# GLA recurrence and SoLU block on one core: a group's first scores moved to another PSUM bank, weight conversion shifted by half a piece, and alpha's transposes moved forward

## The chip, the core and the metric

The kernel runs on one core of a Trainium2 chip. The metric is the device time of one execution in microseconds (us). Six runs of the kernel before gave 390.94 to 396.51 us, with a median of 394.48 us. One further execution was profiled: it took 391.19 us, of which 389.3 us lie between its first and its last instruction. All times inside the kernel below are counted from the first instruction of that execution.

Five engines work side by side, each through its own queue: TensorE (PE) multiplies matrices into PSUM banks, VectorE (DVE), ScalarE (ACT) and GpSimd (POOL) work element by element, and SyncE (SP) issues most of the DMA transfers.

## The reference

Inputs are q, k, v and alpha, each of 4 batches, 8 heads, 768 positions and 48 features, and the weights of a feed-forward block with a hidden width of 1024.

```python
for t in range(S):
    state = alpha[:, :, t, :, None] * state + np.einsum('bhd,bhe->bhde', k[:, :, t], v[:, :, t])
    y[:, :, t] = np.einsum('bhd,bhde->bhe', q[:, :, t], state)
...
x = np.ascontiguousarray(attn_out.transpose(0, 2, 1, 3)).reshape(B * S, H * D)
...
h = x @ w_in
h_max = np.max(h, axis=-1, keepdims=True)
e = np.exp(h - h_max)
sm = e / (np.sum(e, axis=-1, keepdims=True) + 1e-09)
solu = h * sm
mu = np.mean(solu, axis=-1, keepdims=True)
var = np.mean((solu - mu) ** 2, axis=-1, keepdims=True)
ln = (solu - mu) / np.sqrt(var + 1e-06) * g_ln
return (ln @ w_out).astype(np.float32)
```

The first part is a linear attention whose state decays by alpha; the second is an up projection, the product of h and its softmax, a normalisation over the hidden width, and a down projection.

## The kernel before: how it is tiled and ordered

The 768 positions are cut into 6 **groups** of 128. In a group, all 4 batches and 8 heads are worked on together: the running products of alpha are made by scans (`scan_back`, `scan_on`), they scale the transposed keys (`kT`) and queries (`qv`, and `qe` for the last 16 features of each head), and the scores of 4 heads at a time (`scores(g, half)`) are made by 64 small matmuls into four PSUM banks `a[0]` to `a[3]`, one for each batch. `masked(half)` multiplies the four banks by a triangular mask on DVE and so writes `sT`. Then the old state (`read_state`) and the values (`read_values`) are added up in PSUM and copied to `x`.

The feed-forward block of a group runs over 8 **blocks** f of 128 hidden units. `up_mm(g, f)` makes h of 512 tokens on PE, in one of the two banks of the pool `ps_h`. `up_act(g, f)` then issues three operations: e = exp(h) on ACT (L403), u = h*e on DVE (L404), and u2 = u*u on ACT (L405). The next block but one can only be written into the bank when L404 has read it. For group 0 the sums of e and u2 over the blocks are made on PE by `array_sums`, after the fourth and the eighth block. `down(n, half)` multiplies u by half of `w_out`; n counts batches of 128 tokens, and `finish(n)` scales and stores.

The schedule is written out by hand: every engine executes its instructions in the order in which the Python code issues them, and waits on semaphores for what the others must have done. A tile of a pool waits until the tile that held its bank has been read.

**Conversion of the weights.** The weights come as 64-bit floats. They are fetched in 8 **pieces** (`fetch`, onto the slots of the tile `room`; 0 to 3 belong to `w_in`, 4 to 7 to `w_out`), and made into 32-bit floats by `bits(i)` on DVE. It has two halves: part 0 is L594 and L597 (`top`), part 1 is L602, L605 and L606 (`low`, and the sum). `in_range(i)` squares and exponentiates a piece on ACT for a later check (L581, L582), and `scaled(i)` multiplies two blocks of `w_out` by the gains (L613). A slot may be fetched into again when `bits` and `in_range` have read it. Pieces 2 and 3 share slots 1 and 2.

**The stretch that the change touches** is the script between lines 712 and 809, which runs once: the 8 up blocks of group 0 (32 to 60 us), in whose shadow pieces 2 to 5 are converted and the inputs of group 1 are fetched, and then the preparation of group 1 (60 to 112 us). In the loop of the 8 up blocks, part f % 2 of piece 2 + f // 2 is converted after block f. Behind odd blocks (1, 3, 5) ACT has an `in_range` to do. After the loop come `bits(6)`, `bits(7)`, the token sums, the transposes of alpha (`alpha_T(1)`, two DVE transposes at L195 and L198, and a small memset on POOL), and then, three times, a backward scan followed by a product with the transposed keys `tk[i]`. On PE, group 0's `down` runs in pieces between the transposes of keys (`tk`) and queries (`tq`), the mean of `w_out` (`mean`), and `keys_back`. The queries `tq[0]` and `tq[1]` are held in the banks a0 and a1 until DVE multiplies them into `qv` (L780), `tq[1]` last of all. `scores(1, 0)` then takes a0 to a3 anew.

From line 813 on, groups 2 to 5 are worked off by a table (`attend`), which calls `alpha_T` too.

Of the kernel before, what the change touches and what calls it, by code (L numbers as in the profile page):

```python
# [32 lines left out]
def fast_path(ctx, tc, q, k, v, alpha, moe_w_in, moe_w_out, moe_g_ln, out):  # L33
# [12 lines left out]
    nc = tc.nc  # L46
    B, H, S, D = q.shape
# [5 lines left out]
    NB = H + NP  # L53
# [8 lines left out]
    def pool(name, bufs, **kw):  # L62
        return ctx.enter_context(tc.tile_pool(name=name, bufs=bufs, **kw))
# [8 lines left out]
    ps_h = pool("ps_h", 2, space=PS)  # L72
    ps_o = pool("ps_o", 2, space=PS)
    ps_a = pool("ps_a", 1, space=PS)
# [25 lines left out]
    an = const.tile([P, H, TQ, D], FP, name="an")  # L100
    qn = const.tile([P, H, TQ, D], FP, name="qn")
# [16 lines left out]
    SW = P + 1  # L118
    aT = const.tile([P, NB, SW], FP, name="aT")
# [25 lines left out]
    def by_token(x):  # L145

        return x.rearrange("p h u d -> p (h u d)").rearrange("p (b h d) -> p b h d", b=B, h=H)
# [9 lines left out]
    def ends_of(src, tag=None):  # L157

        ends = ring.tile([P, T4], FP, name=tag) if tag else two.tile([P, T4], FP, tag="two", name="ends")
        ends = ends.rearrange("p (b d) -> p b d", b=B)  # L160
        nc.scalar.copy(out=ends.rearrange("p b (h d) -> p b h d", h=H), in_=by_token(src)[:, :, :, E0:D])
        return ends
# [31 lines left out]
    def firsts(src, dst):  # L194
        nc.vector.transpose(out=dst.rearrange("p h (t u) -> p h u t", u=TQ), in_=src[:, :, :, 0:E0])  # L195

    def lasts(src, dst):
        nc.vector.transpose(  # L198
            out=dst.rearrange("p j (i t u) -> p u j i t", u=TQ, i=2),
            in_=src[:, :, :, E0:D].rearrange("p (j i) u d -> p u j i d", i=2),  # L200
        )

    def alpha_T(g):
        nc.gpsimd.memset(aT[:, :, 0:1], 0.0)
        firsts(an, aT[:, 0:H, 1:SW])
        lasts(an, aT[:, H:NB, 1:SW])

    def alpha_over(g):
        x = an.rearrange("p h u d -> p (h u d)")
# [60 lines left out]
    def quarter(b):  # L270
        return slice(32 * b, 32 * b + 32)

    def banks(name, shape, n=B):
        return [ps_a.tile([P] + shape, FP, tag=f"a{b}", name=f"{name}{b}") for b in range(n)]

    def scores(g, half, a=None):
        a = a or banks("a", [NP, P])
        for i in range(NP):
            h = half * NP + i
            for kb, qb in ((h, h), (H + h // 2, H + h)):  # L280
                for b in range(B):
                    nc.tensor.matmul(  # L282
                        a[b][:, i], lhsT=kT[quarter(b), kb], rhs=qv[quarter(b), qb], start=kb == h, stop=kb != h,
                        tile_position=(32 * b, 0), skip_group_check=True,
                    )
        masks[half] = a
# [98 lines left out]
    def up_mm(g, f):  # L385
        d = gr[g]
        h = ps_h.tile([P, T4], FP, tag="h", name="h")
        for a in range(KC):
            nc.tensor.matmul(  # L389
                h, lhsT=w_in[:, a, f * P : (f + 1) * P], rhs=d["x"][:, a].rearrange("p b t -> p (b t)"),  # L390
                start=(a == 0), stop=(a == KC - 1),
            )
        d["h"] = h
# [29 lines left out]
    def array_sums(g, half):  # L423


        d = gr[g]
        if half == 0:
            d["q"] = [ps_a.tile([P, T4], FP, tag=f"a{i}", name=f"quarters{i}") for i in range(2)]
        for i in range(2):
            for f in range(4):  # L430
                r = quarter(f)
                nc.tensor.matmul(
                    d["q"][i][r], lhsT=ones[:, 0:32], rhs=d[4 * half + f][i], start=half == 0, stop=half == 1,
                    tile_position=(0, r.start), skip_group_check=True,
                )
        if half:
            d["p"] = one.tile([P, 2, T4], FP, name="p")
            for i in range(2):
                nc.scalar.copy(out=d["p"][:, i], in_=d["q"][i])
            d["unit"] = small_ones  # L440
# [104 lines left out]
    def place(i):  # L545
        kind, f = pieces[i]
        return w_out[:, f : f + 2, 0:DM] if kind else w_in[:, :, f * P : f * P + 2 * P]
# [3 lines left out]
    def fetch(i, slot, n=1):  # L551

        kind, f = pieces[i]
        w = n * F // (2 if kind else KC)
        raw = room[:, 1536 * slot : 1536 * (slot + n)].bitcast(U32).rearrange("p (c f w) -> p c f w", f=w, w=2)
        if kind:
            parts = [(slice(0, P), c, moe_w_out[(f + c) * P : (f + c + 1) * P, :]) for c in range(2)]
        else:
            rows = moe_w_in[:, f * P : f * P + w].rearrange("(h d) f -> h d f", d=D)
            parts = [(slice(E0 * r, E0 * r + E0), c, rows[NP * c + r, 0:E0]) for c in range(2) for r in range(NP)]  # L560
            parts += [(slice(E1 * h, E1 * h + E1), 2, rows[h, E0:D]) for h in range(H)]
        for rows, c, src in parts:
            if float64:
                nc.sync.dma_start(out=raw[rows, c].rearrange("p f w -> p (f w)"), in_=src.bitcast(U32))  # L564
            else:
                dst = w_out[rows, f + c, 0:DM] if kind else w_in[rows, c, f * P : f * P + w]
                nc.sync.dma_start(out=dst, in_=src)
        for m in range(n):
            raws[i + m] = raw[:, :, w // n * m : w // n * (m + 1)]
# [14 lines left out]
    def bits(i, part=None):  # L584
        if not float64:
            return
        lo, hi = raws[i][:, :, :, 0], raws[i][:, :, :, 1]
        if part != 1:
            made[i] = [
                two.tile([P, F], FP, tag="two", name=x).rearrange("p (c f) -> p c f", c=hi.shape[1])  # L590
                for x in ("top", "low")
            ]
            top = made[i][0].bitcast(U32)
            nc.vector.tensor_scalar(  # L594
                out=top, in0=hi, scalar1=3, scalar2=0x3FFFFFF8, op0=ALU.logical_shift_left, op1=ALU.bitwise_and
            )
            nc.vector.scalar_tensor_tensor(  # L597
                out=top, in0=hi, scalar=0xC0000000, in1=top, op0=ALU.bitwise_and, op1=ALU.bitwise_or
            )
        if part != 0:  # L600
            top, low = made.pop(i)
            nc.vector.tensor_scalar(  # L602
                out=low.bitcast(U32), in0=top.bitcast(U32), scalar1=0xFF800000, scalar2=None, op0=ALU.bitwise_and
            )
            nc.vector.scalar_tensor_tensor(out=low, in0=lo, scalar=2.0**-52, in1=low, op0=ALU.mult, op1=ALU.mult)  # L605
            nc.vector.tensor_tensor(out=place(i), in0=low, in1=top, op=ALU.add)  # L606

    def scaled(i):

        f = pieces[i][1]  # L610
        for c in range(f, f + 2):
            w = w_out[:, c, 0:DM]
            nc.scalar.mul(out=w, in_=w, mul=g_col[:, c : c + 1])  # L613
# [55 lines left out]
    def three(name, where):  # L669
        return [pool.tile([P, NP, P], FP, tag=tag, name=f"{name}{i}") for i, (pool, tag) in enumerate(where)]  # L670
# [12 lines left out]
    for i in range(3):  # L683
        part = slice(NP * i, NP * i + NP)
# [4 lines left out]
    for i in (2, 0, 1):  # L689
        if i == 1:  # L690
            scan_on(0, i)
        part = slice(NP * i, NP * i + NP)
# [17 lines left out]
    in_range(1)  # L710

    for f in range(FC):
        p = 2 + f // 2
        up_mm(0, f)
        if f == 4:
            array_sums(0, 0)
        up_act(0, f)
        bits(p, f % 2)
        if f == 0:
            next_state(0)  # L720
            fetch(4, 3)
            load_first(k, kn, 1)
            load_first(q, qn, 1)
            load(alpha, an, 1)
        elif f == 1:
            in_range(2)
        elif f == 2:
            ends_k = ends_of(kn, "e")
        elif f == 3:
            in_range(3)  # L730
            ends_q = ends_of(qn, "u2")
        elif f == 4:
            fetch(5, 1)
            fetch(6, 2)
        elif f == 5:
            in_range(4)
            fetch(7, 3)
            load_v(1)
        elif f == 6:
            scaled(4)  # L740
        elif f == 7:
            scaled(5)
    bits(6)
    tk = three("tp_k", [(ps_a, "a2"), (ps_a, "a3"), (ps_h, "h")])
    turned(kn, ends_k, tk)
    load(k, kn, 2)
# [2 lines left out]
    scaled(6)  # L749
    bits(7)  # L750
    token_sums(0)
    alpha_T(1)
    down(1, 0)
    scaled(7)
    tq = three("tp_q", [(ps_a, "a0"), (ps_a, "a1")])
# [3 lines left out]
    for i in range(3):  # L759
        scan_back(1, i)  # L760
        part = slice(NP * i, NP * i + NP)
# [15 lines left out]
    for i in range(2):  # L777
        scan_on(1, i)
        part = slice(NP * i, NP * i + NP)
        nc.vector.tensor_tensor(out=qv[:, part], in0=tq[i], in1=aT[:, part, 1:SW], op=ALU.mult)  # L780
    down(2, 0)
    scores(1, 0)
    finish(1)
    alpha_over(1)
    load(alpha, an, 2)
# [3 lines left out]
    masked(1)  # L789
    finish(2)  # L790
    alpha_T(2)
    read_begin()
    for batches in ((0, 1), (2, 3)):
# [82 lines left out]
    for g in range(1, G + 1):  # L876
# [10 lines left out]
        for s in range(FC):  # L887
# [17 lines left out]
            if step:  # L905
                n, half = step
# [499 lines left out]
```

## Time and profile before

| what | us |
|---|---|
| median of 6 runs | 394.48 |
| the profiled execution | 391.19 |
| its span | 389.3 |
| PE busy in the span | 370.8 (95%) |
| DVE busy in the span | 250.5 (64%) |
| ACT busy in the span | 143.9 (37%) |
| 30 to 60 us: PE, DVE, ACT busy | 28.75, 25.48, 22.52 |
| 60 to 90 us: PE, DVE, ACT busy | 25.26, 28.42, 15.01 |
| share of DMA engines busy, 30 to 60 us | 0.89 |

A row of the timeline gives start and duration in us, engine, source line, operation, output <- inputs with their shapes, how many instructions were merged into the row, and in square brackets how long the engine stood idle just before and what ended the wait. Rows of one engine can overlap a little[...]. The chain of waits follows the execution back from its last instruction, at each step to what released it; its shares say on which engine and line the span was spent.

### The profile page before, as it was taken

Reading aid. Unit: us, or ns where it says so; the run is one execution under the profiler, and the core shown is the slowest. Engines: PE = TensorE matmul, PEld = TensorE weight load, DVE = VectorE, ACT = ScalarE, POOL = GpSimd, SP = SyncE. Lnnn points to the kernel's source line nnn. Section 1 sums busy time; section 2 is a strip of 40 time slices with the busy share of each in tenths; the row PEclk is TensorE's granted clock in tenths of the full one; section 3 lists DMA queues with packets and bytes.
Section 4 is the critical chain, followed back from the end, with each engine's and each line's share of the span. In section 5 each row is a group of like instructions: output and inputs, shape, how many; then the busy total and the mean of one; then the engine's idle time right before and its main releaser. Section 6 shows DMA issues by size and latency. Waiting matters only on the chain.

```text
span 389.3 us, 10598 instructions
## 1 busy us (share of the span) xinstructions
PE 370.8 (95%) x4661; PEld 224.1 (58%) x4661; DVE 250.5 (64%) x417; ACT 143.9 (37%) x252; POOL 125.0 (32%) x135
## 2 busy tenths in 40 slices
PE   8698999787999999999999999999999999999995
PEld 8685345455665556556656556566555575555552
DVE  0989888996987857694655893665895511444410
ACT  2628775553424325224253215153123231333111
POOL 4020000041042993337423436422635620333210
PEclk9989999999899999999999999999999999999999
DMA  9975989403446300674000764000600000000011
GB/s 183 195 192 158 231 269 163 94 20 86 111 113 83 83 3 3 82 184 102 22 2 24 112 155 101 22 3 22 101 2 22 22 24 2 20 21 21 22 43 48
DMA packets 86567, 30.79 MB, mean 79 GB/s; under 512 B 68072, under 2 KB 84720, under 8 KB 86512
## 3 DMA queue, kind: packets, MB, share of 16 engines
q1 hardware_dynamic: 85488, 29.11, 34.7%
q10 hardware_dynamic: 1024, 0.92, 0.7%
q8 instruction: 38, 0.62, 0.7%
q14 instruction: 17, 0.14, 0.1%
HBM read 25.30 MB, written 4.72 MB: 77 GB/s over the span
## 4 chain that ended last, share of the span: by engine, by line
PE 71%; DVE 12%; DMA 6%; ACT 5%; SPq 3%; issue 2%; DVEq 0%
PE o L500 30%; PE h L389 24%; PE y L314 9%; PE a L282 5%; DMA room<-in_v_dram 3%; SPq L152 2%; DMA room<-in_moe_w_in_dram 2%; DVE room L404 2%; PE kv L364 1%; ACT sq L581 1%; DVE aT L220 1%; SPq L564 1%; DMA kn<-in_k_dram 1%; DVE top L597 1%; DVE hT L220 1%
## 5 line engine op out<-in xcount | busy, mean ns | idle before, releaser
L500 PE MATMUL o<-w_out,room 128*128 128x385 f32 x384 | 135.0, 496 | 1.1 <-DVE least L234 1.1
L389 PE MATMUL h<-x,w_in 128*128 128x512 f32 x288 | 132.2, 598 | 1.2 <-DVE g_col L618 1.2
L500 PEld LDWEIGHTS o<-w_out,room 128*128 128x128 f32 x384 | 72.1, 192 | 58.1 <-issue 17.2
L389 PEld LDWEIGHTS h<-x,w_in 128*128 128x128 f32 x288 | 53.0, 189 | 59.9 <-issue 48.7
L404 DVE TENSOR_TENSOR room<-h,e 128x512 f32<-128x512 f32 x40 | 27.8, 694 | 83.0 <-ACT e L403 82.8
L403 ACT ACTIVATE e<-h 128x512 f32<-128x512 f32 x40 | 23.9, 598 | 105.5 <-PE h L389 105.5
L530 POOL TENSOR_TENSOR r<-sums,mhalf 128x1 f32<-128x1 f32 x20 | 14.3, 716 | 138.8 <-DVE sums L522 138.8
L420 POOL TENSOR_TENSOR p<-p,e 128x512 f32<-128x512 f32 x30 | 41.8, 1392 | 15.7 <-ACT e L403 15.6
L405 ACT ACTIVATE u<-room 128x512 f32<-128x512 f32 x40 | 25.2, 630 | 42.3 <-DVE room L404 42.3
L293 DVE TENSOR_TENSOR sT<-a,mask 128x512 f32<-128x512 f32 x44 | 27.3, 681 | 10.1 <-PE a L282 10.1
L282 PE MATMUL a<-qv,kT 32*128 32x128 f32 x704 | 27.7, 290 | 4.3 <-DVE least L234 1.9
L282 PEld LDWEIGHTS a<-qv,kT 32*128 32x128 f32 x704 | 24.2, 197 | 11.8 <-issue 4.0
L220 DVE TENSOR_TENSOR_SCAN hT<-aT,unit 128x516 f32<-128x516 f32 x18 | 23.1, 1337 | 8.6 <-ACT aT L677 8.5
L420 DVE TENSOR_TENSOR p<-p,u 128x512 f32<-128x512 f32 x30 | 23.2, 775 | 6.5 <-ACT u L405 6.5
L244 POOL TENSOR_TENSOR kT<-kT,hT 128x1024 f32<-128x1024 f32 (+1 forms) x8 | 13.3, 1685 | 42.8 <-DVE kT L195 42.8
L314 PE MATMUL y<-sT,vn 128*32 128x128 f32 x768 | 23.2, 274 | 2.0 <-issue 1.2
L220 DVE TENSOR_TENSOR_SCAN aT<-aT,seed 128x516 f32<-128x516 f32 x18 | 23.0, 1278 | 0.6
L314 PEld LDWEIGHTS y<-sT,vn 128*32 128x32 f32 x768 | 20.8, 110 | 3.9 <-issue 2.7
L212 ACT ACTIVATE sq<-an,mone 128x1536 uint8<-128x1536 f32 x12 | 18.8, 1570 | 0.2
L314 PE MATMUL y<-qv,state 32*32 32x128 f32 x960 | 16.9, 277 | 1.0 <-DVE sT L293 0.9
L314 PEld LDWEIGHTS y<-qv,state 32*32 32x32 f32 x960 | 12.1, 103 | 7.9 <-issue 5.4
L532 ACT ACTIVATE o_sb<-o,r 128x384 f32<-128x384 f32 x16 | 9.3, 582 | 18.8 <-POOL r L530 18.8
(141 smaller groups left out, 377.9 us busy)
## 6 DMA issues: line engine op xcount, KB each, us to landing
an<-in_alpha_dram SPq DMA_DIRECT2D x20, 192.0 KB, 4.8
out_dram<-o_sb SPq DMA_DIRECT2D x20, 192.0 KB, 1.9
room<-in_moe_w_out_dram SPq DMA_DIRECT2D x8, 384.0 KB, 4.8
kn<-in_k_dram SPq DMA_DIRECT2D x16, 192.0 KB, 4.1
qn<-in_q_dram SPq DMA_DIRECT2D x16, 192.0 KB, 4.1
vn<-in_v_dram SPq DMA_DIRECT2D x10, 256.0 KB, 3.9
room<-in_moe_w_in_dram SPq DMA_DIRECT2D x16, 128.0 KB, 3.9
kn<-in_k_dram SPq DMA_DIRECT2D x4, 384.0 KB, 5.8
```

What stands on the lines that cost most here:

```text
L212: nc.scalar.activation(out=sq, in_=x, func=AF.Relu, scale=sign, bias=mone, accum_out=over[:, g, i : i + 1])
L220: nc.vector.tensor_tensor_scan(out=o, data0=a, data1=s, initial=1.0, op0=ALU.mult, op1=ALU.add)
L282: nc.tensor.matmul(a[b][:, i], lhsT=kT[quarter(b), kb], rhs=qv[quarter(b), qb], start=kb == h, stop=kb != h, tile_position=(32 * b, 0), sk ...
L293: nc.vector.tensor_tensor(out=sT[:, b, half * NP : half * NP + NP], in0=a[b], in1=mask[:, None, :].to_broadcast([P, NP, P]), op=ALU.mult,)
L314: nc.tensor.matmul(y_bank(b)[quarter(r), a], lhsT=lhsT, rhs=rhs, start=(b, r) not in begun, stop=stop, tile_position=(row, 32 * r), skip_g ...
L389: nc.tensor.matmul(h, lhsT=w_in[:, a, f * P : (f + 1) * P], rhs=d["x"][:, a].rearrange("p b t -> p (b t)"), start=(a == 0), stop=(a == KC ...
L403: nc.scalar.activation(out=e, in_=h, func=AF.Exp)
L404: nc.vector.tensor_tensor(out=u, in0=h, in1=e, op=ALU.mult)
L405: nc.scalar.activation(out=u2, in_=u, func=AF.Square)
L420: eng.tensor_tensor(out=p, in0=d[0][i] if f == 1 else p, in1=d[f][i], op=ALU.add)
L500: nc.tensor.matmul(d["o"][:, 0 : DM + 1], lhsT=u_of(g, f)[:, b * P : b * P + P], rhs=w_out[:, f], start=(f == 0), stop=(f == FC - 1), skip ...
L530: nc.gpsimd.tensor_tensor(out=r, in0=s[:, 3:4], in1=mhalf, op=ALU.pow)
```

## The change

Four things are done, all of them in the order of the hand-written script; no operation is added or taken out.

1. In the loop of group 0's up blocks, both halves of piece 2 are converted after block 0, and from then on the conversion is half a piece ahead: part 0 of the next piece after odd blocks, part 1 after even ones. Piece 6's first half is converted after block 7, and only its second half after the loop.
2. `alpha_T` can be called in two parts. Part 0 is the memset and the transpose of the last 16 features (L198), part 1 the transpose of the first 32 (L195). For group 1, part 0 is issued after block 6, and part 1 after block 7, between the two halves of piece 6. For the other groups the two transposes change places.
3. `fetch(5, 1)` and `fetch(6, 2)` are issued after block 3, ahead of the copy `ends_q`, instead of after block 4.
4. `scores(1, 0)` gets a bank of `ps_h` in place of a1.

```diff
-    def alpha_T(g):
-        nc.gpsimd.memset(aT[:, :, 0:1], 0.0)
-        firsts(an, aT[:, 0:H, 1:SW])
-        lasts(an, aT[:, H:NB, 1:SW])
+    def alpha_T(g, part=None):
+        if part != 1:
+            nc.gpsimd.memset(aT[:, :, 0:1], 0.0)
+            lasts(an, aT[:, H:NB, 1:SW])
+        if part != 0:
+            firsts(an, aT[:, 0:H, 1:SW])
...
     for f in range(FC):
-        p = 2 + f // 2
         up_mm(0, f)
         if f == 4:
             array_sums(0, 0)
         up_act(0, f)
-        bits(p, f % 2)
+
+        for half in (0, 1) if f == 0 else (f + 1,):
+            bits(2 + half // 2, half % 2)
...
         elif f == 3:
             in_range(3)
-            ends_q = ends_of(qn, "u2")
-        elif f == 4:
             fetch(5, 1)
             fetch(6, 2)
+            ends_q = ends_of(qn, "u2")
...
         elif f == 6:
             scaled(4)
+            alpha_T(1, 0)
         elif f == 7:
             scaled(5)
-    bits(6)
+            alpha_T(1, 1)
+    bits(6, 1)
...
     token_sums(0)
-    alpha_T(1)
     down(1, 0)
...
     down(2, 0)
-    scores(1, 0)
+
+    scores(1, 0, three("a", [(ps_a, "a0"), (ps_h, "h"), (ps_a, "a2"), (ps_a, "a3")]))
     finish(1)
```

## The prediction

> **What bounds the kernel now.** I read the page's busy shares first, then the chain of waits, then the timelines of DVE, ACT and PE over 30 to 97 us, where the edits lie. The page's chain shows where the whole span goes:
>
> ```profile
> PE 71%; DVE 12%; DMA 6%; ACT 5%; SPq 3%; issue 2%; DVEq 0%
> ```
>
> PE carries most of it, but the 12% of DVE and 5% of ACT lie largely in the script changed here: listed in time, the chain runs over ACT and DVE from 41 to 61 us, over DVE alone from 61 to 88.6 us, and then over PE. What changes DVE before 88.6 us can therefore reach the end, and whether it does is decided by PE's waits.
>
> DVE's timeline in the up loop of group 0 (L404 reads the bank h):
>
> ```profile
> 40.20 0.69 DVE L404 TENSOR_TENSOR room<-h,sT 128x512 f32<-128x512 f32 x1 [0.80 <-ACT sT L403]
> ...
> 43.95 0.69 DVE L404 TENSOR_TENSOR room<-h,sT 128x512 f32<-128x512 f32 x1 [0.61 <-ACT sT L403]
> ...
> 46.41 0.68 DVE L404 TENSOR_TENSOR room<-h,sT 128x512 f32<-128x512 f32 x1
> ...
> 50.71 0.69 DVE L404 TENSOR_TENSOR room<-h,sT 128x512 f32<-128x512 f32 x1 [1.15 <-ACT sT L403]
> ...
> 52.83 0.69 DVE L404 TENSOR_TENSOR room<-h,sT 128x512 f32<-128x512 f32 x1
> ...
> 56.57 0.69 DVE L404 TENSOR_TENSOR room<-h,sT 128x512 f32<-128x512 f32 x1 [0.60 <-ACT sT L403]
> ```
>
> These are the products of blocks 1 to 6. The step from an odd to an even block is long (3.75, 4.30, 3.74 us) and ends in a wait on ACT; the one from even to odd is short (2.46, 2.12 us) and has no wait. ACT says why:
>
> ```profile
> 40.92 0.63 ACT L405 ACTIVATE sT<-room 128x512 f32<-128x512 f32 x1 [0.76 <-DVE room L404]
> 41.46 0.91 ACT L581 ACTIVATE sq<-room 128x768 f32<-128x768 f32 x1
> 42.27 0.19 ACT L581 ACTIVATION_READ_ACCUMULATOR sq<-room 128x1 f32 x1
> 42.49 0.84 ACT L582 ACTIVATE sq<-sq 128x768 f32<-128x768 f32 x1
> 43.24 0.19 ACT L582 ACTIVATION_READ_ACCUMULATOR sq<-sq 128x1 f32 x1
> 43.34 0.58 ACT L403 ACTIVATE sT<-h 128x512 f32<-128x512 f32 x1
> ```
>
> Block 1's square waits for block 1's product, the range check of a piece (1.88 us) follows, and block 2's exponential stands behind it. So after an odd block the next product can't start before 3.75 us, whatever DVE does. DVE idles 0.80 + 0.61 + 1.15 + 0.60 + 0.73 = 3.89 us in the loop, and not at all from there to 89.5 us.
>
> PE, where the scores begin:
>
> ```profile
> 83.91 2.83 PE L500 MATMUL o<-w_out,room 128*128 128x385 f32 x8 [1.08 <-DVE least L234]
> 86.67 0.48 PE L282 MATMUL a<-qv,kT 32*128 32x128 f32 x2
> 88.63 2.06 PE L282 MATMUL a<-qv,kT 32*128 32x128 f32 x62 [1.48 <-DVE qv L780]
> ```
>
> Two score matmuls go at 86.67, and the third waits until bank a1 is free, 1.96 us. Before that PE also waits for the token sums at 71.11 (0.97 us), at 76.17 (0.64), 77.65 (0.57) and at 83.91 (1.08).
>
> **What the Trainium skill says.** "PSUM — Partial Sum Buffer", section PSUM bank collisions, asks that PSUM be guarded by bank, not by address; the wait at 88.63 is such a guard, and the trace agrees: it ends with the L780 that reads a1, though the scores of that half need only the L780 before it. The same page, section Engine vs sequencer instructions, has ScalarE and VectorE queues as strict FIFO; the trace agrees at 43.34, where an exponential whose h was ready stands behind the range check. "TensorE: Matmul & The Clock Gate", Part 1, lets PE fall to half its clock in free-running windows of about 3.4 us after low activity; the trace agrees once: from 98.00 to 103.20 us the mean granted clock is 0.67. That is a lottery of about 1.7 us a window, which I add to the range, not to the sum.
>
> **The change part by part.** Durations are those of the profiled execution.
>
> *Half a piece ahead.* Part 0 costs DVE 1.86 us for pieces 2 and 3 (L594 to the next product, 44.55 to 46.41) and 1.51 for later ones; part 1 costs 2.46; a product 0.61. Before, the long part 1 stood in the long ACT step and the short part 0 in the short one. The change swaps them: after odd blocks there is now 0.61 + 1.86 or 1.51 of DVE work in a step of 3.75 us, and after even ones 0.61 + 2.46 = 3.07 us in a step that took 2.1 to 2.5. The product starts, walked forward from block 0 (36.83, unmoved):
>
> - block 1: 36.83 + 0.61 + 1.97 + 2.45 (both halves of piece 2) = 41.86, before 40.20;
> - block 2: + 3.75 = 45.6; block 3: + 3.07 = 48.67; block 4: + 4.30 = 52.97;
> - block 5: + 3.07 = 56.04; block 6: + 3.74 = 59.78, before 56.57;
> - block 7: + 3.07 + 1.0 (the small transpose, L198) = 63.85, before 59.46.
>
> So piece 2's haste is paid at block 1, and the idle time isn't filled but moved. PE is late with it: block 4 needs the bank that product 2 releases at 46.3 (it began at 44.69), block 7 begins at about 56.75 instead of 54.6, and the second quarter sums end at 65.3 instead of 61.9. That has cover: PE waits for DVE at 71.11 anyway.
>
> *Alpha's transposes.* L195 (1.92 us to the next start) and L198 (1.0) leave the stretch behind the token sums and enter the one ahead. After block 7: 63.85 + 0.61 + 1.49 (piece 6, part 0) + 1.92 (L195) + 2.46 + 4.05 (piece 7) = 74.38 for the token sums' transpose, against 70.61: **3.77 us later**. The scans begin at 75.35 against 74.44, 0.91 later: 2.92 of the 3.77 was only moved. The POOL memset has nothing in front of it for 60 us; it costs nothing.
>
> *Fetches.* SP's order stays. Its fetch of piece 5 waits for the range check of piece 3, as now (48.74), and goes at about 51.0. Landing took 4.8 to 5.1 us, so it is there at 56 to 56.6, just when DVE wants it (56.65). Up to 1.6 us more would hide in DVE's wait for block 6. Pieces 6 and 7 land before 58.5 and 63, used at 64.5 and 70. The value, key and query fetches queued behind move 2 to 3 us and are read after 100 us. Cost 0.
>
> *PE after the loop.* The mean of w_out waits for the token sums: 71.11 + 3.77 = 74.88. Half a down follows, then the mean's second matmul (ACT's two range checks and its copy move alike): 79.94 to 80.85. The bank of the last query transposes is another one in the program as built: they wait for the third key product, 80.35 + 0.91 = 81.26. Then without a gap: transposes 1.0, down 2.7, keys back 1.45, down 2.8, so scores at **89.25**. The wait of 1.08 at 83.91 is gone.
>
> *The bank.* The scores need qv of heads 0 to 3 (86.7 on DVE) and ACT's masked copies of qe (key copies from 85.65, 1.44, then two copies 1.35: 88.45). The wait of 1.96 us for a1 is gone, but PE itself comes only at 89.25. What is late next is thus PE, not DVE.
>
> *Sum.* Scores begin at 89.25 instead of 88.63: **+0.62 us**. In pieces: + 3.77 (token sums) - 0.12 (tighter waits from 76 to 81 us) - 1.08 - 1.96 = 0.61. From there on the chain is PE's, and DVE's alpha for group 2 moves by 0.9, a like amount, so the end moves by 0.6. The bounds: if the loop gains idle time, each us is a us at the end; if it loses some, the end can fall by 3.5 us at most, since PE's work from 57.24 to the scores is 26.6 us plus 1.2 us of the mean's two waits: 85.1 against 88.63. 391.19 + 0.6 = 391.8 for this execution. The median of the six runs lies 3.3 us above it, and the change does nothing to that: 394.48 + 0.6 = **395.1 us**.
>
> **Rivals.** *The idle time is filled* (for it: 3.89 us idle, 2.92 moved into it; against it: the ACT step of 3.75 us begins at the very product that is now later). If the loop's end moved by the transposes' time or less, the scores would begin between 85.1 and 88.4: 391.0 to 394.2 us.
>
> *The loop stretches further, and the end is clearly later.* Place: the odd-to-even steps, where the product, ACT and the bank of h form a ring, and piece 5's landing. Price: one for one. It decides from the point where the token sums come more than 3.1 us late, since PE has only the waits 1.08 and 1.96 to give; at 7.1 us late the loss passes 1%. For it: the walk has already used up all cover; DMA engines are 0.89 busy there. Against: every duration in the walk is measured in the same loop. 396.5 to 400 us.
>
> *The scores don't come sooner*, because ACT's copies of qe (88.45) end after PE's arrival: 0.8 us of play, then one for one; 395 to 396.
>
> **How the numbers follow.** A measurement of this kernel can tell about 1%, here 3.9 us. The forecast has 0.60 (own range 393.5 to 396.5, with the lottery), the filled idle time 0.18, the stretched loop 0.18, the late copies 0.04. Of the first and the last nearly nothing leaves 1%; of the filled case about a third, helped by a clock window less; of the stretched one about two thirds. So faster 0.07, same 0.80, slower 0.13. The range takes in the upper two thirds of the filled case and most of the stretched one: 392.0 to 398.5.
>
> **What would show it.** Right: products of blocks 1 to 7 near 41.9, 45.6, 48.7, 53.0, 56.0, 59.8, 63.9; waits of L404 on ACT only at even blocks, longer than now (1.3 to 2.2 us); no wait at all before the odd ones; the token sums' transpose near 74.4, the scans near 75.4; the 1.08 and 1.96 us waits on PE gone and the scores near 89.3. Wrong: block 7's product before 62.5 or the token sums before 73.4 (then the filled case), or after 75.5 (then the stretched one); a wait of L594 on a DMA of w_out of more than 1.6 us; a wait at the scores on ACT's L248.

## The result and the profile after

The changed kernel takes 392.26 us (median of 34 runs, 390.42 to 394.11), the kernel before 392.93 us (71 runs, 389.16 to 398.18). The ratio is 1.0004 with a 95% interval of 0.9989 to 1.002, which is +0.16 us (-0.43 to +0.79): **no change that can be measured**. Of the 71 times of the kernel before 24 lie above 395 us, as do three of the six shown at first and none of the changed kernel's; the ratio is made without these, so that its level for the kernel before is 392.26 / 1.0004 = 392.1 us.

The profiled execution took 392.40 us, with a span of 390.5. Its chain of waits has nearly the old shares:

```profile
PE 73%; DVE 11%; SPq 7%; DMA 3%; ACT 3%; issue 2%; ACTq 0%; DVEq 0%
```

DVE's timeline in the up loop of group 0, the rows of the product u = h*e (now L406; two lines were added above it), columns as before:

```profile
41.86 0.68 DVE L406 TENSOR_TENSOR room<-h,sT 128x512 f32<-128x512 f32 x1
...
45.61 0.69 DVE L406 TENSOR_TENSOR room<-h,sT 128x512 f32<-128x512 f32 x1 [1.21 <-ACT sT L405]
...
48.67 0.68 DVE L406 TENSOR_TENSOR room<-h,sT 128x512 f32<-128x512 f32 x1
...
52.98 0.69 DVE L406 TENSOR_TENSOR room<-h,sT 128x512 f32<-128x512 f32 x1 [2.16 <-ACT sT L405]
...
56.04 0.68 DVE L406 TENSOR_TENSOR room<-h,sT 128x512 f32<-128x512 f32 x1
...
59.78 0.69 DVE L406 TENSOR_TENSOR room<-h,sT 128x512 f32<-128x512 f32 x1 [1.59 <-ACT sT L405]
```

These are blocks 1 to 6. The waits on ACT now stand at the even blocks alone (before, blocks 1 and 7 had one too), but there are 4.96 us of them in place of 3.89, and every product is later than it was. ACT's timeline between blocks 3 and 4 gives the reason:

```profile
49.39 0.63 ACT L407 ACTIVATE sT<-room 128x512 f32<-128x512 f32 x1 [1.42 <-DVE room L406]
49.92 0.96 ACT L583 ACTIVATE sq<-room 128x768 f32<-128x768 f32 x1
...
51.01 0.84 ACT L584 ACTIVATE sq<-sq 128x768 f32<-128x768 f32 x1
...
51.85 0.60 ACT L161 COPY u<-qn 128x512 f32<-128x512 f32 x1
52.36 0.59 ACT L405 ACTIVATE sT<-h 128x512 f32<-128x512 f32 x1
```

The odd block's square starts 1.42 us later than ACT was free for it, because DVE had the long half of the conversion to do first. The range check follows it, and the exponential of block 4 comes after both. The two long pieces of work, DVE's and ACT's, now stand one behind the other instead of side by side.

PE, from the last query transposes (L170) to group 1's first up block:

```profile
81.25 1.08 PE L170 MATMUL tp_q<-ident,u 128*32 128x128 f32 x32 [0.47 <-DVE kT L765]
...
84.96 1.47 PE L303 MATMUL tp<-ident,kT 128*128 128x128 f32 x12
86.27 2.76 PE L502 MATMUL o<-w_out,room 128*128 128x385 f32 x8
88.96 2.07 PE L284 MATMUL a<-qv,kT 32*128 32x128 f32 x64
...
99.11 4.28 PE L502 MATMUL o<-w_out,room 128*128 128x385 f32 x8
...
112.92 2.74 PE L391 MATMUL h<-x,w_in 128*128 128x512 f32 x6
```

Both old waits of PE, 1.08 us ahead of the down and 1.48 within the scores, are gone, and yet the scores begin at 88.96 us instead of 88.63. Group 1's first up block begins at 112.92 instead of 112.32, 0.60 us later, and the span is 1.2 us longer. The row of the kernel before:

```profile
112.32 2.74 PE L389 MATMUL h<-x,w_in 128*128 128x512 f32 x6
```

The down at 99.11 takes 4.28 us where others take 2.86, since PE ran at half its clock for 3.4 us (granted 0.50); it did so at the same place in the first profile of the kernel before (4.38 us at 98.68).

### The profile page after: what moved, and what is told of

It reads as the page before. It is cut to its first block, busy times and chain, and to the rows that moved or that the text cites. A ratio compares the mean times of both kernels' runs of the same rounds, so it can differ in the third digit from the quotient of the medians.

```text
span 390.5 us, 10600 instructions
## 1 busy us (share of the span) xinstructions
PE 372.0 (95%) x4661; PEld 223.9 (57%) x4661; DVE 250.6 (64%) x417; ACT 143.8 (37%) x252; POOL 125.5 (32%) x135
## 4 chain that ended last, share of the span: by engine, by line
PE 73%; DVE 11%; SPq 7%; DMA 3%; ACT 3%; issue 2%; ACTq 0%; DVEq 0%
PE o L502 31%; PE h L391 24%; PE y L316 9%; PE a L284 5%; SPq L566 4%; SPq L152 2%; DMA room<-in_moe_w_in_dram 2%; DVE room L406 2%; PE kv L366 1%; DVE low L607 1%; PE tp L303 1%; DVE sT L295 1%; DVE hT L222 1%; DMA room<-in_moe_w_out_dram 1%; ACT sq L583 1%
## 5 line engine op out<-in xcount | busy, mean ns | idle before, releaser
L406 DVE TENSOR_TENSOR room<-h,e 128x512 f32<-128x512 f32 x40 | 27.7, 693 | 82.6 <-ACT e L405 82.5
```

Of the source, the lines that this page charges most:

```text
L406: nc.vector.tensor_tensor(out=u, in0=h, in1=e, op=ALU.mult)
```

## The experiments

In the expectations **theory A** is the account on record: the times of the loop as walked there, and from the scores on one for one to the end. D, N and T came later and are told where they first appear; B and C are told in the expectations that name them.

### The bank alone

```diff
 # the kernel before
-    scores(1, 0)
+    scores(1, 0, three("a", [(ps_a, "a0"), (ps_h, "h"), (ps_a, "a2"), (ps_a, "a3")]))
```

> The kernel before with one edit: the first scores of group 1 take a bank of ps_h in place of a1. Theory A (the walk of the prediction, one part alone): nothing ahead of the scores moves, the 64 score matmuls run at once behind the down that ends at 86.7 us, so they start at 86.7 instead of 88.6 us (the two early ones aside), and the whole kernel is 1.9 us faster (about 0.5%). Theory B (the wait is only replaced): the scores stay at about 88.6 us on another wait, or the mask on DVE holds the second scores so that they start at 93.4 us as before, and the time is the same within 0.3 us.

Measured: 393.47 us (14 runs), ratio 0.9999 (0.9966 to 1.0032). The scores did come at 86.75, 1.88 us sooner, as A had it, and the time didn't follow; B had the time right but not its reason. Further down this run's timeline of PE shows group 1's first two up blocks and the third:

```profile
108.20 2.74 PE L389 MATMUL h<-x,w_in 128*128 128x512 f32 x6
...
112.35 2.84 PE L389 MATMUL h<-x,w_in 128*128 128x512 f32 x6
117.56 2.84 PE L389 MATMUL h<-x,w_in 128*128 128x512 f32 x6 [2.37 <-DVE room L404]
```

PE arrives early and then waits 2.37 us for DVE. DVE's timeline has the cause 17 us ahead of that, where alpha of group 2 is transposed. The first row is the kernel before, the second this run:

```profile
99.22 2.04 DVE L195 STREAM_TRANSPOSE aT<-an 128x1024 f32<-128x1024 f32 x1 [0.27 <-DMA an<-in_alpha_dram]
```

```profile
100.13 2.17 DVE L195 STREAM_TRANSPOSE aT<-an 128x1024 f32<-128x1024 f32 x1 [2.69 <-DMA an<-in_alpha_dram]
```

The load is issued by SP only at 93.69, because it waits until ACT's sums over the old alpha (L212) have read the tile, and these stand in ACT's queue behind `finish(1)`:

```profile
90.31 1.56 ACT L212 ACTIVATE sq<-an,mone 128x1536 uint8<-128x1536 f32 x1
...
92.00 1.57 ACT L212 ACTIVATE sq<-an,mone 128x1536 uint8<-128x1536 f32 x1
```

The gain meets a second bound, which runs over ACT, a DMA and DVE, and which the sooner scores don't move.

### Two other parts of the change, and the range checks

Old order of the conversion, with alpha early and the bank kept:

```diff
 # the changed kernel
-        for half in (0, 1) if f == 0 else (f + 1,):
-            bits(2 + half // 2, half % 2)
+        bits(2 + f // 2, f % 2)
...
-    bits(6, 1)
+    bits(6)
```

> The changed kernel with the conversion back in its old order (part f % 2 of piece 2 + f // 2), alpha's transposes behind blocks 6 and 7 and the new bank kept. Theory A: the products of blocks 1 to 6 are where they are in the kernel before (40.2, 44.0, 46.4, 50.7, 52.8, 56.6), block 7 at 59.7, the token sums' transpose at 72.8, the scans at 73.7, the third query transposes at 79.7, the scores at 87.6 us: 1.0 us before the kernel before and 1.3 us before the changed one. Theory C (the half piece ahead fills idle time and helps): the scores come later than in the changed kernel (89.0 us).

Measured: 391.57 us (22 runs), ratio 0.9958 (0.9928 to 0.9989). In this execution the work began later, and PE ran at half its clock at the loop's start; from the loop's first product to the scores it took 51.43 us, against 52.15 in the changed kernel and 51.80 in the kernel before. The half clock is in that 51.43: block 1's product came 4.18 us behind the first one instead of 3.37. Without these 0.81 us the scores would come at 50.6, an estimate, 1.2 us before the kernel before where A had 1.0. So half a piece ahead costs what the other edits bring. The earlier fetches, and the changed order of the two transposes in groups 2 to 5, were not taken back alone.

Alpha's transposes back behind the token sums, the rest of the change kept:

```diff
 # the changed kernel
-            alpha_T(1, 0)
...
-            alpha_T(1, 1)
...
     token_sums(0)
+    alpha_T(1)
```

> The changed kernel with alpha's two transposes back behind the token sums, the conversion half a piece ahead and the new bank kept. Theory A: block 7's product at 62.8, the token sums' transpose at 71.5, the scans at 75.3 as in the changed kernel, but PE's chain from the mean of w_out on is 2.9 us earlier, the third query transposes at 78.4, keys back at 82.2, the down of tokens 256 to 383 at 84.7 (waiting for DVE's finish), the scores at 87.4 us: 1.5 us before the changed kernel, though the same DVE work is done. Theory D (alpha's early transposes are what gives): the scores at 89.0 us or later.

Measured: 393.67 us (22 runs), ratio 1.0031 (1.0011 to 1.0052). (The "theory D" of this expectation is not the D further down.) The scores come at 88.04, sooner than in the changed kernel, though later than A's 87.4, and the time is longer. A and the scores alone can't give that. What is later here is DVE: its backward scans begin at 75.77 instead of 75.27, its transposes of group 2's alpha at 102.23 instead of 100.32, behind a wait of 3.49 us on their load, and PE waits 1.50 us for DVE at group 1's third up block.

The range checks on the side of the long half, which tests the ring of ACT and DVE named in the prediction:

```diff
 # the changed kernel
             load(alpha, an, 1)
-        elif f == 1:
             in_range(2)
         elif f == 2:
-            ends_k = ends_of(kn, "e")
-        elif f == 3:
             in_range(3)
             fetch(5, 1)
+        elif f == 3:
             fetch(6, 2)
-            ends_q = ends_of(qn, "u2")
-        elif f == 5:
+            ends_k = ends_of(kn, "e")
+        elif f == 4:
             in_range(4)
+        elif f == 5:
+            ends_q = ends_of(qn, "u2")
             fetch(7, 3)
             load_v(1)
```

> The changed kernel with ACT's range checks of pieces 2, 3 and 4 moved from behind blocks 1, 3, 5 to behind blocks 0, 2, 4, and the two copies of keys' and queries' ends from behind blocks 2, 3 to behind 3, 5; nothing else. Theory A (the long DVE half and the long ACT step should stand in one step): products of blocks 1 to 7 at 41.9, 44.3, 48.1, 50.5, 54.2, 56.6, 60.7 instead of 41.9, 45.6, 48.7, 53.0, 56.0, 59.8, 63.8; the token sums' transpose at 71.2, the scans at 72.1, the scores at 85.8 us, 3.2 us before the changed kernel and 2.9 before the kernel before. Theory C (ACT is not what holds the products): products and scores within 0.5 us of the changed kernel.

Measured: 388.80 us (6 runs), ratio 0.9897 (0.9854 to 0.9941), 1% under both kernels. DVE's products of blocks 1 to 6 in this run:

```profile
42.02 0.68 DVE L406 TENSOR_TENSOR room<-h,sT 128x512 f32<-128x512 f32 x1
...
44.47 0.68 DVE L406 TENSOR_TENSOR room<-h,sT 128x512 f32<-128x512 f32 x1
...
48.21 0.69 DVE L406 TENSOR_TENSOR room<-h,sT 128x512 f32<-128x512 f32 x1 [0.60 <-ACT sT L405]
...
50.60 0.69 DVE L406 TENSOR_TENSOR room<-h,sT 128x512 f32<-128x512 f32 x1 [0.22 <-ACT sT L405]
...
54.41 0.69 DVE L406 TENSOR_TENSOR room<-h,sT 128x512 f32<-128x512 f32 x1 [0.67 <-ACT sT L405]
...
56.81 0.69 DVE L406 TENSOR_TENSOR room<-h,sT 128x512 f32<-128x512 f32 x1 [0.24 <-ACT sT L405]
```

Three waits of 1.2 to 2.2 us have become four of 0.2 to 0.7, and the token sums come at 71.34 instead of 74.30, the scores at 86.00 instead of 88.96; all of A's times are met within 0.25 us. No operation differs from the changed kernel, only which step of ACT shares a block with which half of DVE's. Piece 5 is also fetched a block sooner, but no conversion waited for a fetch in either run. So the pairing of ACT's and DVE's long pieces is **shown** as what held the products.

### Is the second bound the load of alpha?

Theory **D**: the end follows DVE's line, which hangs on the load of group 2's alpha. Theory **N**: the place of the stretch at half clock decides. Four kernels, each with the same edit:

```diff
     mean(1)
+    alpha_over(1)
...
     load(q, qn, 2)
+    load(alpha, an, 2)
...
     finish(1)
-    alpha_over(1)
-    load(alpha, an, 2)
```

With the bank, in the kernel before:

> The kernel before, with the bank change alone and, new, group 2's alpha loaded sooner: ScalarE's two overflow sums over alpha of group 1 (L212) stand right behind the second mean (L635, 77.6 us in the kernel before, where ScalarE then idles to 81.99), and SP's load of alpha for group 2 right behind the load of q. Theory D (the end follows VectorE's line, which in e1_bank_alone stood 2.69 us before group 2's alpha transposes for the load): load issued at 80 to 81.5 instead of 93.7, no wait for the transfer, the transposes of group 2's alpha start at 97.2 to 97.8 instead of 100.13, the wait of 2.37 us for VectorE's room in group 1's third block is gone or under 0.5; time 1.5 to 2.4 us under the kernel before, ratio 0.994 to 0.996. Theory A (the time follows the scores): scores at 86.7 as in e1_bank_alone, so the same time as there, ratio 1.000. Theory N (the place of the half-clock stretch decides): no relation to either, a ratio within 0.997 to 1.003 that follows whether a stretch falls near 98 us.

Measured: 387.69 us (6 runs, 386.86 to 393.18), ratio 0.99 (0.9847 to 0.9953). SP issues the load at 81.56, DVE's timeline shows no wait ahead of the transposes, and PE's has the first three up blocks of group 1 without the 2.37 us. First DVE, then PE:

```profile
97.94 2.09 DVE L195 STREAM_TRANSPOSE aT<-an 128x1024 f32<-128x1024 f32 x1
```

```profile
108.97 2.74 PE L389 MATMUL h<-x,w_in 128*128 128x512 f32 x6
...
113.12 5.42 PE L389 MATMUL h<-x,w_in 128*128 128x512 f32 x12
```

Without the bank:

> The kernel before with only the earlier load of group 2's alpha (overflow sums behind the second mean, load behind that of q), no bank change. Theory D: VectorE's wait for this load was only 0.27 us in the kernel before, so the transposes start at 98.9 to 99.0 instead of 99.22 and the time falls by at most 0.3 us, ratio 0.999 to 1.000; the load matters only together with the bank. Theory A: scores at 88.63 as before, ratio 1.000. If the ratio is 0.996 or lower, the load bounded more than that wait, and D's sum is wrong.

Measured: 392.13 us (22 runs), ratio 1.0011 (0.9983 to 1.0039). Neither the bank alone (0.9999) nor the load alone (1.0011) moves the time; both together take 1% off. That one alone does nothing and both do something is D's forecast and neither A's nor N's; the size is more than the 0.994 to 0.996 that D gave.

In the kernel with the checks on even blocks, and in the changed kernel:

> e5_checks_on_even (the changed kernel with ScalarE's range checks behind even blocks, ratio 0.9897) plus the earlier load of group 2's alpha. Theory D: the wait of 1.02 us for the load ahead of the transposes of group 2's alpha goes, and only it: the transposes at 96.3 instead of 97.35, time 0.8 to 1.1 us under e5, near 387.8, ratio 0.986 to 0.988. Theory A: as e5, 0.990.

> The changed kernel plus the earlier load of group 2's alpha, nothing else. Theory D: its wait of 1.03 us ahead of the transposes of group 2's alpha goes, these start at 99.3 instead of 100.32, and the time falls by 0.7 to 1.1 us against the changed kernel (392.26), to 391.3, ratio to the kernel before 0.997 to 0.9985. Theory A: scores at 88.96 as in the changed kernel, ratio 1.000.

Measured: 388.57 us (21 runs), ratio 0.9921 (0.9896 to 0.9946), and 391.83 us (22 runs), ratio 0.9998 (0.9976 to 1.0019). D's waits went as it said: the transposes begin without one, at 97.05 and 99.39 us. The times D named did not come: in the first its 0.986 to 0.988 is excluded, in the second its 0.997 to 0.9985 lies at the interval's edge, and A's 0.990 and 1.000 fit. In these two, PE's up block of group 1 comes late by itself (73.37 and 75.87 us in the table below), and where PE is the later one, a sooner DVE is worth nothing. So D was half the account.

### Two lines

Theory **T** joins the two: group 1's up blocks start when PE gets there, and the third waits for DVE if DVE is later still. The profiles of all runs, read in that way (us from the loop's first product, since the executions begin at different times):

| kernel | half clock near 98 us | scores begin | alpha of group 2 transposed (DVE) | first up block (PE) | third waits for DVE | end | end less the last two |
|---|---|---|---|---|---|---|---|
| before | yes | 51.80 | 62.39 | 75.49 | - | 352.47 | 276.98 |
| changed | yes | 52.15 | 63.51 | 76.11 | - | 353.69 | 277.58 |
| bank alone | no | 49.87 | 63.25 | 71.32 | 2.37 | 351.42 | 277.73 |
| no half ahead | no | 51.43 | 62.79 | 72.69 | 0.81 | 351.88 | 278.38 |
| alpha back | yes | 51.17 | 65.36 | 74.58 | 1.50 | 354.03 | 277.95 |
| checks on even | yes | 49.06 | 60.41 | 73.04 | - | 349.96 | 276.92 |
| bank and load | no | 49.89 | 60.50 | 71.53 | - | 348.96 | 277.43 |
| load alone | no | 51.82 | 62.06 | 73.36 | - | 350.58 | 277.22 |
| even and load | yes | 49.03 | 59.28 | 73.37 | - | 350.83 | 277.46 |
| changed and load | yes | 52.13 | 62.38 | 75.87 | - | 353.19 | 277.32 |

(Where two scores went ahead, the other 62 are meant.) The last column stays within 276.9 to 278.4 while the end moves over 5 us. What follows the first up block takes the same time in all of them, within 1.5 us, so the end is settled there, by one line or the other. The column of the scores doesn't order the ends; a stretch at half clock between them and the up block sets it back by about 2.2 us on average (23.41 to 24.34 us from the scores to the up block in the six profiles with it, 21.26 to 22.14 in the eight without, those below taken in).

T was then tried on what the bank is worth when alpha is early, without it:

> The kernel before with group 1's alpha transposes beside the loop's last blocks alone: no bank, conversions in the old order. It is e3_no_half_ahead without its bank. Theory T (two lines: the end stands 277.0 to 277.7 us behind the start of group 1's first up block on TensorE, plus any wait of TensorE there for VectorE's room): the scores issue 2 matmuls where e3 issued 64 and the other 62 wait for the second query product, 0.5 to 0.7 us later than e3's, against a slack of about 0.8 that e3 showed as a wait for VectorE; ratio 0.996 to 0.9975. Theory A (one for one with the scores, and the bank worth 1.96 us as in the forecast): 1.96 us above e3, ratio 1.0005 to 1.001.

> The changed kernel with group 1's first scores in their old banks. Theory T: two scores at 88.96, the other 62 at 89.4 to 89.6 behind the second query product, so TensorE 0.5 to 0.6 us later from there; ratio to the kernel before 1.0005 to 1.002 (the changed kernel 1.0004). Theory A with the bank worth its whole former wait of 1.96: scores at 90.9, ratio 1.005.

The first is the run without half ahead with `scores(1, 0)` in its old banks, the second the changed kernel with the same. Measured: 391.99 us (22 runs), ratio 0.9982 (0.9958 to 1.0007), and 392.91 us (14 runs), ratio 1.0009 (0.9981 to 1.0038). The times can't tell T and A apart in the first, and exclude A's 1.005 in the second. The timeline of PE in the second has the size:

```profile
88.97 2.57 PE L284 MATMUL a<-qv,kT 32*128 32x128 f32 x64
```

The scores take 2.57 us instead of 2.07: the bank a1 is free half a microsecond after PE comes. The first ends at 277.26 us behind its up block, the second at 277.98, just over T's 277.0 to 277.7.

### The better version, and the kernel before once more

> e6_bank_and_early_load once more, since its 6 times (386.86 to 388.19, and 393.18) leave an interval of 1%. Theory T: in its profile TensorE's first up block of group 1 starts 71.5 us behind the loop's first product, with no wait for VectorE's room over 0.5 us, and the end 277.0 to 277.7 us behind that; in the times a ratio of 0.989 to 0.995. If e6 was luck, the ratio is 0.996 or above.

> The kernel before itself, unchanged, timed as any other: a look at what two times of one kernel differ by, and a second profile of it. Ratio 1.000 with an interval of 0.3% to each side; median between 391.9 and 393.2, so about 2 us under the 394.48 of the six times shown at first. Theory N (the half-clock stretch near 98 us is drawn anew in each execution): it may be absent here, and then group 1's first up block starts 2.1 to 2.4 us sooner behind the loop's first product than the 75.49 us of the first profile; if it belongs to the kernel, 75.3 to 75.7 again.

Measured: the bank with the earlier load again 388.85 us (6 runs), ratio 0.9895 (0.9849 to 0.9941); its up block came 72.37 us behind the first product, not T's 71.5, with PE at half clock at the loop's start, and the end 277.67 behind that. The kernel before 392.79 us (22 runs), ratio 0.9995 (0.997 to 1.0019), end 277.60 us behind the up block. So the gain stands, and the level of 394.48 does not. The two profiles without half clock near 98 us in the same place give 1.6 us of gain (350.58 with the load alone, 348.96 with both), less than the 4 us of the times.

The granted clock, which is on record for every run as its mean over the execution, tells more. Average times of the runs with 0.993 or more, each session with its own runs of the kernel before:

| session | the kernel before | one part alone | both |
|---|---|---|---|
| first (bank alone) | 391.17 (5 of 53 runs) | 392.48 (5 of 14) | |
| second (load alone, both) | 390.21 (15 of 58) | 390.45 (4 of 22) | 387.54 (5 of 6) |
| third (both again) | 390.86 (5 of 51) | | 388.72 (6 of 6) |

At a like clock both edits together are worth 2.1 to 2.7 us, near D's 1.5 to 2.4, and either alone takes nothing off. The rest of the 4 us goes with the clock: 11 of the 12 runs with both have the high one (the twelfth, 393.18 us, has 0.986), and most runs of the kernel before don't. The groups are small, and why the version with both is held back by the clock less often isn't shown.

The second profile of the kernel before answers N. Busy times by stretch, first of the first profile, then of the second; the columns are the stretch, its length, busy PE, PE's weight loads, DVE, ACT and POOL with their instructions, granted clock, share of DMA engines busy and GB/s:

```profile
94.90:98.30 3.40, 2.41 (x131) 1.98 (x128) 2.74 (x7) 0.00 (x0) 0.00 (x0) 1.00 0.97 225
98.30:101.70 3.40, 3.40 (x29) 1.86 (x12) 3.13 (x4) 2.58 (x4) 0.60 (x2) 0.51 0.16 59
```

```profile
98.60:102.00 3.40, 2.41 (x129) 1.98 (x128) 2.71 (x6) 0.00 (x0) 0.00 (x0) 1.00 0.94 221
102.00:105.40 3.40, 3.40 (x58) 1.85 (x52) 2.93 (x4) 2.54 (x4) 0.60 (x2) 1.00 0.19 65
```

One program, the same work of PE in the stretch ahead (2.41 us of 3.40), and half the clock in one execution and the full clock in the other. From the 62 scores to the up block it took 23.69 us in the first (88.63 to 112.32) and in the second 21.33, 2.36 less:

```profile
92.37 2.06 PE L282 MATMUL a<-qv,kT 32*128 32x128 f32 x62 [1.47 <-DVE sums L517]
...
113.70 2.74 PE L389 MATMUL h<-x,w_in 128*128 128x512 f32 x6
```

The Trainium skill ("TensorE: Matmul & The Clock Gate", Part 1) calls the window in which activity is judged free-running; that agrees with one program being struck in one execution and not in another. Counted from the loop's first product the up block came at 74.12, only 1.37 us sooner than 75.49 and not N's 2.1 to 2.4, because in this execution PE ran at half its clock at the loop's start and the scores were 0.99 later. N is thus no rival to T, but a draw of 2.4 us on PE's line in each execution.

## Why the prediction was right or wrong

**The loop** was right to the step. The forecast had the products of blocks 1 to 7 at 41.9, 45.6, 48.7, 53.0, 56.0, 59.8 and 63.9; they came at 41.86, 45.61, 48.67, 52.98, 56.04, 59.78 and 63.84. Token sums at 74.30 (forecast 74.38), scans at 75.27 (75.35). The checks on even blocks show that the cause was the right one, and the filled and the stretched rivals are out. One sum is off by a little: the walk has 2.92 us "only moved" and the scans 0.91 later, while 3.77 - 2.92 is 0.85; the two transposes took 2.86 from 71.58 to 74.44.

**PE after the loop** was right in its order. The last query transposes began at 81.25, behind the third key product as forecast (81.26). The two waits went, and ACT's copies of qe made no new one. Piece 5's fetch went at 51.01 and no conversion waited for it, as forecast. The wait for a1 was read as a guard by bank and not by address; the trace can't tell these apart, since the queries and the scores both fill the bank with the same 128x512 floats.

**The step that failed** is the sum, in two of its sizes: the change's and the level's. The forecast of 395.1 is 2.84 us above the 392.26 measured. Of that 0.46 are the change, 0.62 forecast against 0.16 measured (-0.43 to +0.79), and 2.38 are the level, 394.48 against 392.1.

*The change.* The term that was too large is PE's run to the scores: "Then without a gap: transposes 1.0, down 2.7, keys back 1.45, down 2.8, so scores at **89.25**". It took 7.71 us where 7.99 are needed for 89.25 (the four terms add up to 7.95). Keys back and the last down were put in with their whole rows. When the next row follows at once it begins before the one ahead ends: from start to start they took 1.31 (84.96 to 86.27) and 2.69 (86.27 to 88.96). So the scores came 0.33 us later and not 0.62, and nearly half of the forecast change was never there. That the up block of this pair came 0.60 later, as forecast for the end, is luck: 0.27 of it arose behind the scores, where a pause of PE put down to issue was 1.24 us instead of 0.86. Between 0.33 and 0.62 at the end the measured interval doesn't decide.

*The level.* "The median of the six runs lies 3.3 us above it, and the change does nothing to that": the six times spread from 390.94 to 396.51 with three above 395.9, and their median fell in the gap between 393.04 and 395.92, where none of them lay. A forecast of a small difference took this for the centre; the kernel before timed again gave 392.79. None of the changed kernel's 34 times lies above 394.11; why not isn't shown.

**"From there on the chain is PE's"** was not tested by the pair, where PE was the later line, and is wrong as a rule. The sentence beside it, that DVE's alpha for group 2 moves "a like amount", passed over the wait of 0.27 us on the load that the profile of before already had ahead of that transpose: DVE's line had its own bound, the load behind ACT's sums, and was close behind PE's. The bank alone shows it (PE 1.88 us sooner, time the same), alpha back shows it the other way (scores 0.92 us sooner than in the changed kernel, time longer). The bank's term in the sum, 1.96 us, is the size of a wait in the kernel before; in the changed kernel the bank is worth 0.5.

The range of 392.0 to 398.5 held the result, near its lower end, and "within 1%" was the likeliest case.

## What to carry to other kernels

When an engine's wait is taken away, ask which other engine would be waited for at the next place where the two meet, and expect from one of the two alone no more than what the other leaves free there: here the bank (0.9999) and the load (1.0011) were worth nothing one at a time and 1% together, of which 2.1 to 2.7 us stand at a like clock. When rows that follow at once are added up, use the steps from start to start. Where conversion or checking is shared out over a loop, pair the long piece of one in-order engine with the long piece of the other in the same step, not in alternate ones. And look at the single times before anchoring a forecast on their median: six of them in two clumps have it where none of them lies.

## What the runs showed of the hardware that was not expected

- A stretch at half clock, 3.4 us in the kernel before, followed work in which PE was busy 2.41 to 2.57 us of 3.40, mostly in 32x32 tiles, in six of the fourteen profiled executions, and followed the same work in the same program once and not the other time. Between the two profiles of that program it cost PE 2.4 us up to the next up block, more than half of 3.4: 0.86 us of it is a pause of PE in the middle of the values, put down to issue, which the profile without the stretch doesn't have. Over all profiles this pause is 0.27 to 1.57 us with the stretch and 0 to 0.45 without.
- The stretch near 98 us is not the only one. The first profile of the kernel before has another from 20.0 to 23.4 us (granted 0.50 to 0.53), which the prediction passed over, and its second profile has one from about 32.4 to 39.3 us, at the loop's start, which the first lacks.
- DVE's wait for alpha of group 2 was not for a slow transfer. In the run with the bank alone the four transfers, of 192 KB each, were issued one after another from 93.7 to 95.1 us and landed 3.0 to 4.1 us after their issue, less than the median of 4.7 over all loads of alpha on that run's page. DVE began on them at 100.13, 6.4 us after the first issue.
